# Layer norm's shift made on POOL, and work placed anew around the attention of a two-layer linear-attention and MLP kernel

## The chip, the cores and the metric

The kernel runs on one core of a Trainium2 chip. The core has a tensor engine (PE, with its weight loads PEld), a vector engine (DVE), a scalar engine (ACT), a general one (POOL) and a queue that issues most transfers (SP); each works through its own instructions in order, and they wait for each other by semaphores. The metric is the time of one execution in microseconds (us); of several runs, the median. Time before: 2634.08 us, median of 3 runs (2633.55 to 2637.23).

## The reference

Two layers, each an attention (A) and an MLP (B), both with a residual, with the same weights in both layers. S = 2048 rows, D = 576, H = 32 heads of Dh = 18, F = 4608, all in fp32.

```python
def _A_ref(x, wqkv, w_phi, wo):
    qkv = (x @ wqkv).reshape(B, S, 3, H, Dh).transpose(2, 0, 3, 1, 4)
    q, k, v = qkv[0], qkv[1], qkv[2]
    pq = jnp.einsum("bhsd,hdf->bhsf", q, w_phi)
    pk = jnp.einsum("bhsd,hdf->bhsf", k, w_phi)
    phi_q = concatenate([softmax(pq), softmax(-pq)])
    phi_k = concatenate([softmax(pk), softmax(-pk)])
    kv = jnp.einsum("bhsf,bhsd->bhfd", phi_k, v)
    z = jnp.einsum("bhsf->bhf", phi_k)
    num = jnp.einsum("bhqf,bhfd->bhqd", phi_q, kv)
    den = jnp.einsum("bhqf,bhf->bhq", phi_q, z)[..., None] + 1e-6
    return (num / den).transpose(0, 2, 1, 3).reshape(B, S, D) @ wo

def _B_ref(x, w1, b1, w2, b2):
    r = relu(x @ w1 + b1)
    return (r * r) @ w2 + b2

x = A_x
for layer in range(2):
    x = x + _A_ref(_layernorm(x), A_wqkv, A_w_phi, A_wo)
    x = x + _B_ref(_layernorm(x), B_w1, B_b1, B_w2, B_b2)
```

The attention isn't causal: the sums kv and z run over all 2048 rows, so no row's attention can be finished before the keys and values of every row are in.

## The kernel before

**Tiling.** The rows are cut into 4 blocks of 512, a block into 4 tiles of 128 rows (one row per partition). Products are made in three matmuls, of a high and a low piece of each fp32 operand (high by high, high by low, low by high); names end in h and l for them. PE writes into banks of its accumulators; ACT copies a result's high piece from there, and DVE subtracts it for the low one.

**Names.** A name's last number is left out in the profile. n_3m is the mean and variance of a tile of block 3 (blocks and tiles count from 0, over all blocks the tiles from 0 to 15), n_3d the inverse deviation, n_3b the shift (minus mean times inverse deviation), n_3n the normalised tile, n_3p its transpose in a bank, n_3h and n_3l the two pieces of the block's transposed rows. s0K9m is the peaks (largest and smallest per head) of the keys of tile 9, s0K9e the exponentials of both signs, s0K9r their sums. s010v is the values of tile 10, kvp the bank in which the sums over keys (kv) come together, zb the sums z spread over the partitions, t0q3Q0e to t0q3Q3e the query features of the last block's four tiles; t0ow0m and t0ow2m the products of these with zb for the first and second pair of tiles. Names with t1 or s1 are those of the second layer.

**A norm.** `Norm.stats` makes mean and variance on DVE (L353, L354) and the inverse deviation on POOL in two operations (L355, L356). `Norm.shift` makes the shift on DVE (L335). `scale_by_act` normalises on ACT (L344, L345) with shift and inverse deviation as its operands. `turn` transposes on PE (L380), ACT copies the high piece (L381), DVE makes the low one (L382); `rest` does the same for the last 64 columns of two tiles (L389 to L391).

**The stages**, with their places in the profile of before. *Fold* (0 to 44 us): the map w_phi is multiplied into the weights of queries and keys, while the four tiles of the first block are normalised. *Opening* (44 to about 240): for each of 16 tiles its keys (projection L421, copy L445, peaks L457 and L458, difference L471 with one half on DVE and one on POOL for the first twelve, exponentials L481 on ACT, sums L484, reciprocals L485, scaling L494), its values (L437; two columns of constants by memsets on POOL, L428 and L429), the sum of their product into kvp (L521), and the queries of the last block; beside them the norms of the remaining 12 tiles. *First barrier* (to about 308): the last keys, `key_totals` (z, L538 to L546), `key_blocks` (kv in block form, L557 to L571), the `Weights` of the first two tiles and of the other two (features times zb, L590; sums, L595; the denominator's reciprocal into the scaling, L600 to L603; scaling of the features, L494), the heads' products (L626 to L652), the projection with wo (L670, L673) and the norm ahead of the MLP. Then the MLPs of all four blocks, with the attention of the other blocks and the keys of the next layer woven in (to 1440). *Between* (1440 to 1521): the rest of the second layer's keys, values and queries, by `between()`. *Second barrier* (to 1593), and the MLPs of the second layer to the end.

**What sets the order.** In these stages the order of PE, ACT, DVE and POOL is that in which the code calls the operations. In the opening and in between, a table sets it: `plan.on(slot, depth, call, ...)` puts a call into a slot; the slots are run through in order, and within a slot the calls with greater depth come first. Two slots make one unit, a projection in two halves of 288 columns (so a unit is k, v, q or p of one tile). `unit[...]` is the first slot of each, in the order of `line`. The barriers are written out in code; there `halves[i]()` are halves of projections of the following block's queries that give PE something to do. Banks are taken in turn by `wtile`, from the rest of them and those named in `spare`.

## Time and profile before

| | us |
|---|---|
| median of 3 runs | 2634.08 (2633.55 to 2637.23) |
| the profiled execution's own time | 2635.62 |
| its span, first to last instruction | 2633.9 |
| PE busy | 2550.1 (97%) |
| DVE busy | 1179.7 (45%) |
| ACT busy | 745.4 (28%) |
| POOL busy | 87.4 (3%) |
| mean granted clock of PE | 0.989 |

The profile is of one execution. The span leaves out 1.72 us ahead of the first and behind the last instruction. "Busy" counts only instructions that compute, and matmuls are pipelined, so PE at 97% need not be PE at its peak; the granted clock is the share of full speed that PE was given. In rows of the timeline the columns are start, duration, engine, line, operation, output<-inputs with their shapes, count, and in brackets how long the engine had been idle and who released it. In rows of the waits they are engine and operation that waits, whom it waited for, us in total, times, and the longest.

### The profile page before, as it was taken

The numbers are of one execution on the slowest core, as the hardware profiler recorded it, in microseconds if no ns is written. First come the engines' busy times: TensorE is split into PE (matmuls) and PEld (weight loads), VectorE is DVE, ScalarE is ACT, GpSimd is POOL, SyncE is SP. The second block draws the span as 40 slices with busy tenths as digits, with TensorE's granted clock in tenths as the row PEclk, the third lists the DMA queues.
The fourth block names the chain that finished last, engine by engine and source line by source line (L and its number), as shares of the span: only waits on it lengthen the run. The fifth ranks groups of instructions, "written<-read, shape, count | busy, mean of one in ns | idle before, by whom it ended". The sixth has DMA issues, their size and how long they took to land.

```text
span 2633.9 us, 37310 instructions
## 1 busy us (share of the span) xinstructions
PE 2550.1 (97%) x15300; PEld 2241.3 (85%) x15300; DVE 1179.7 (45%) x2017; ACT 745.4 (28%) x1278; POOL 87.4 (3%) x229
## 2 busy tenths in 40 slices
PE   8788899999999999999999989999999999999999
PEld 7788788889888888888888888888888888888887
DVE  5677785543553445434412666431263325432111
ACT  4333444332221222212222333312222222312221
POOL 2110100000000000000000000000000000000000
PEclk9899999999999999999999999999999999999999
DMA  9412386886765766566556226556744574456665
GB/s 303 133 47 72 134 299 230 274 300 204 251 206 179 242 226 205 189 219 198 175 196 212 65 84 193 173 164 201 259 160 148 191 264 152 161 180 223 196 198 170
DMA packets 161143, 505.47 MB, mean 192 GB/s; under 512 B 21334, under 2 KB 49526, under 8 KB 160974
## 3 DMA queue, kind: packets, MB, share of 16 engines
q1 hardware_dynamic: 160974, 503.10, 57.4%
q8 instruction: 121, 1.98, 0.3%
q14 instruction: 48, 0.39, 0.0%
HBM read 418.39 MB, written 84.64 MB: 191 GB/s over the span
## 4 chain that ended last, share of the span: by engine, by line
PE 87%; DVE 5%; ACT 2%; DMA 2%; POOL 1%; issue 1%; SPq 0%; DVEq 0%; ACTq 0%; POOLq 0%
PE m_0ph L795 9%; PE m_1ph L795 9%; PE m_2ph L795 9%; PE m_3ph L795 8%; PE m_0acc L821 7%; PE m_1acc L821 7%; PE m_2acc L821 7%; PE m_3acc L821 6%; PE m_1acc L813 2%; PE m_0acc L813 2%; PE m_2acc L813 2%; PE m_3acc L813 2%; PE a_2po L670 1%; PE a_0po L670 1%; DMA m_3rr<-in_B_w 1%
## 5 line engine op out<-in xcount | busy, mean ns | idle before, releaser
L795 PE MATMUL m_0ph<-a_0nh,m_0h 128*128 128x512 f32 x720 | 226.4, 396 | 0.0
L795 PE MATMUL m_2ph<-a_2nh,m_2h 128*128 128x512 f32 x720 | 225.7, 395 | 0.6 <-DMA m_2h<-dw 0.6
L821 PE MATMUL m_0acc<-m_0s,m_0hb 128*128 128x448 f32 x864 | 189.9, 368 | 0.0
L821 PE MATMUL m_3acc<-m_3s,m_3hb 128*128 128x448 f32 x864 | 189.6, 368 | 0.3 <-DVE m_3hb L805 0.3
L821 PE MATMUL m_1acc<-m_1s,m_1hb 128*128 128x448 f32 x864 | 189.5, 367 | 0.3 <-DVE m_1hb L805 0.3
L821 PE MATMUL m_2acc<-m_2s,m_2hb 128*128 128x448 f32 x864 | 189.6, 368 | 0.0
L821 PEld LDWEIGHTS m_1acc<-m_1s,m_1hb 128*128 128x128 f32 x864 | 161.6, 188 | 18.1 <-DVE m_1hb L805 0.5
L821 PEld LDWEIGHTS m_3acc<-m_3s,m_3hb 128*128 128x128 f32 x864 | 161.4, 188 | 17.5 <-PE m_3ph L795 0.5
L821 PEld LDWEIGHTS m_2acc<-m_2s,m_2hb 128*128 128x128 f32 x864 | 160.7, 188 | 16.0
L821 PEld LDWEIGHTS m_0acc<-m_0s,m_0hb 128*128 128x128 f32 x864 | 160.4, 188 | 15.4
L805 DVE CAST m_2hb<-m_2hr 128x512 fp32r<-128x512 f32 x72 | 30.8, 427 | 316.3 <-ACT m_2hr L802 315.9
L795 PEld LDWEIGHTS m_2ph<-a_2nh,m_2h 128*128 128x128 f32 x720 | 135.5, 188 | 31.2 <-issue 1.0
L795 PEld LDWEIGHTS m_0ph<-a_0nh,m_0h 128*128 128x128 f32 x720 | 135.5, 188 | 29.8
L805 DVE CAST m_1hb<-m_1hr 128x512 fp32r<-128x512 f32 x72 | 30.7, 427 | 269.3 <-ACT m_1hr L802 269.3
L801 ACT ACTIVATE m_2hr<-m_2ph,b1t 128x512 f32<-128x512 f32 x72 | 49.5, 688 | 352.3 <-PE m_2ph L795 346.4
L805 DVE CAST m_0hb<-m_0hr 128x512 fp32r<-128x512 f32 x72 | 30.8, 427 | 260.8 <-ACT m_0hr L802 260.4
L801 ACT ACTIVATE m_0hr<-m_0ph,b1t 128x512 f32<-128x512 f32 x72 | 49.6, 688 | 333.5 <-PE m_0ph L795 333.5
L801 ACT ACTIVATE m_1hr<-m_1ph,b1t 128x512 f32<-128x512 f32 x72 | 49.6, 688 | 322.8 <-PE m_1ph L795 322.8
L795 PE MATMUL m_3ph<-t0onh,m_3h 128*128 128x512 f32 (+1 forms) x380 | 116.7, 391 | 6.3 <-ACT m_3hr L801 3.5
L795 PE MATMUL m_1ph<-t1onh,m_1h 128*128 128x512 f32 (+1 forms) x380 | 115.7, 389 | 0.5 <-ACT t1onh L381 0.5
L795 PE MATMUL m_3ph<-a_3nh,m_3h 128*128 128x512 f32 x360 | 113.3, 396 | 0.4 <-DMA m_3h<-dw 0.4
L795 PE MATMUL m_0ph<-a_0nl,m_0h 128*128 128x512 f32 x288 | 113.1, 393 | 0.0
(1928 smaller groups left out, 5535.1 us busy)
## 6 DMA issues: line engine op xcount, KB each, us to landing
m_2h<-dw SPq DMA_DIRECT2D x72, 640.0 KB
m_0h<-dw SPq DMA_DIRECT2D x72, 640.0 KB
m_1h<-dw SPq DMA_DIRECT2D x72, 640.0 KB
m_2s<-dw SPq DMA_DIRECT2D x72, 576.0 KB
m_0s<-dw SPq DMA_DIRECT2D x72, 576.0 KB
m_1s<-dw SPq DMA_DIRECT2D x72, 576.0 KB
dw<-m_3h SPq DMA_DIRECT2D x36, 640.0 KB
m_3h<-dw SPq DMA_DIRECT2D x36, 640.0 KB
```

What stands on the lines that cost most here:

```text
L670: nc.tensor.matmul(pt[:, :HP], a, m[:w, g], start=(g == 0 and k == 0), stop=(g == NG - 1 and k == 2))
L795: nc.tensor.matmul(ph[:, cols], a, m, start=(k == 0), stop=(k == 3 * KC + 1))
L801: nc.scalar.activation(hr, ph, AF.Relu, bias=b1t[:, f : f + 1])
L805: nc.vector.tensor_copy(hh, hr)
L813: nc.tensor.matmul(acc[KC], a, m, start=(f == 0 and k == 0), stop=(f == NF - 1 and k == 2))
L821: nc.tensor.matmul(acc[t][:, :R], a[:, rows], m, start=(f == 0 and k == 0), stop=(f == NF - 1 and k == 2))
```

## The change

It has five parts.

1. `Norm.shift` runs on POOL instead of DVE. It is used in the fold and the opening (16 tiles), in both barriers (4 each) and in between (4).
2. In the opening, statistics of a tile come one slot later, its scaling one slot later and at a place behind other work of the slot, its transpose two slots later; the first four tiles likewise by less. The sum over keys of a tile comes one or two slots later.
3. In `key_blocks` the product for the last head of each quarter (kq) comes ahead of the two masked ones (ko).
4. In the barrier, the products of the second pair's features with zb are made on POOL, ahead of the first half's heads, the second of them into a spare buffer for exponents. Both sums then follow each other, and the projection of the second tile comes behind the weights.
5. In between, the banks are taken in another order; statistics and shifts are spread over slots 0 and 1 (before: all in 0), scaling stands in slots 2 and 4, transposes in slots 3 and 6, and the sums over keys come one slot later.

```diff
         def shift(self, t):
             mv, rstd = self.stat[t]
             nmr = sb.tile([P, 1], F32, tag="nmr", name=f"{self.name}b{t}")
-            nc.vector.tensor_scalar(nmr, mv[:, 0:1], rstd, -1.0, op0=ALU.mult, op1=ALU.mult)
+            nc.gpsimd.tensor_scalar(nmr, mv[:, 0:1], rstd, -1.0, op0=ALU.mult, op1=ALU.mult)
...
-        def product(self, i):
-            m = self.m[i] = sb.tile([P, 2, D], F32, tag="m", name=f"{self.name}m{i}", bufs=1)
-            nc.vector.tensor_mul(m, self.e[i], self.zb)
+        def product(self, i, engine=nc.vector, spare=False):
+            if spare:
+                m = new_e(f"{self.name}m{i}")
+            else:
+                m = sb.tile([P, 2, D], F32, tag="m", name=f"{self.name}m{i}", bufs=1)
+            self.m[i] = m
+            engine.tensor_mul(m, self.e[i], self.zb)
...
         for t in range(NT):
             out.load(t)
+        w = weights[1]
+        w.product(0, nc.gpsimd)
+        w.product(1, nc.gpsimd, True)
...
         heads(0, 2)
-        w = weights[1]
         norm = Norm(dst, f"{out.name}n")
         next(gen)
-        w.product(0)
         w.total(0)
-        x = out.project(0)
-        w.product(1)
         w.total(1)
-        out.project(1)
+        out.project(0)
         w.both()
         w.apply(0)
         w.apply(1)
+        out.project(1)
         heads(1, 2)
...
         for N in range(NT):
             plan.on(3 * N + 1, 2, stats, N)
-            plan.on(3 * N + 2, 3, scale, N)
-            plan.on(3 * N + 4, -1, turn, N)
+            plan.on(3 * N + 3, -1, scale, N)
+            plan.on(3 * N + 4, -2, turn, N)
...
-                plan.on(max(raw + 7, unit["v", T] + 2), 6, ks.add, T)
+                plan.on(max(raw + 7, unit["v", T] + (3 if T < 13 else 4)), 6, ks.add, T)
         for N in range(NT, NB * NT):
             at = unit["k", N - NT]
             plan.on(at - 4, 9, load_rows, N)
-            plan.on(at + 2, 0, stats, N)
-            plan.on(at + 3, 3, scale, N)
-            plan.on(at + 4, 7, turn, N)
+            plan.on(at + 3, 2.5, stats, N)
+            plan.on(at + 4, 3.5, scale, N)
+            plan.on(at + 6, -1, turn, N)
...
-        spare["tags"] = ["acc1", "acc2", "acc3", "acc4", "h"]
+        spare.update(tags=["h", "acc4", "acc1", "acc2", "acc3"], i=4)
...
-            plan.on(unit["p", t] + 2, 6, ks.add, ("p", t))
+            plan.on(unit["p", t] + 3, 6, ks.add, ("p", t))
...
-                plan.on(max(unit["k", t] + 8, unit["v", t] + 2), 6, ks.add, t)
+                plan.on(max(unit["k", t] + 8, unit["v", t] + 3), 6, ks.add, t)
         for t in range(NT):
-            plan.on(0, 8, norm.stats, t, rows[t])
-            plan.on(0, 8, norm.shift, t)
-            plan.on(0, 7, norm.scale_by_act, t) if t < 2 else plan.on(4, 7, norm.scale_by_act, t)
-            plan.on((3, 3, 5, 6)[t], -1, norm.turn, t)
+            plan.on(t // 2, 8, norm.stats, t, rows[t])
+            plan.on(t // 2, 8, norm.shift, t)
+            plan.on(2 + t // 2 * 2, -1, norm.scale_by_act, t)
+            plan.on(3 + t // 2 * 3, -1, norm.turn, t)
             if t % 2:
-                plan.on((3, 6)[t // 2], -2, norm.rest, t // 2)
+                plan.on(3 + t // 2 * 3, -2, norm.rest, t // 2)
```

What the table makes of it on DVE, in the turn of the keys of tile 9 in the opening. Before:

```order
L457 TENSOR_REDUCE s0K9m<-s0ks_1891 128x32
L458 TENSOR_REDUCE s0K9m<-s0ks_1891 128x32
L353 BN_STATS n_3s_1953<-x_13_1705 128x6 x2
L354 BN_AGGR n_3m_1954<-n_3s_1953 128x2
L335 TENSOR_SCALAR n_3b_1961<-n_3m_1954,n_3d_1955 128x1
L471 TENSOR_TENSOR s0K9e<-s0ks_1891,s0K9m 128x576
L382 TENSOR_TENSOR n_3l<-n_3p_1988,n_3h 128x4x128
L391 TENSOR_TENSOR n_3h<-n_3p_1995,n_3h 64x256
L484 TENSOR_REDUCE s0K9r<-s0K9e 128x64
```

And with the change:

```order
L457 TENSOR_REDUCE s0K9m<-s0ks_1882 128x32
L458 TENSOR_REDUCE s0K9m<-s0ks_1882 128x32
L382 TENSOR_TENSOR n_3l<-n_3p_1946,n_3h 128x4x128
L353 BN_STATS n_3s_1953<-x_13_1702 128x6 x2
L354 BN_AGGR n_3m_1954<-n_3s_1953 128x2
L471 TENSOR_TENSOR s0K9e<-s0ks_1882,s0K9m 128x576
L484 TENSOR_REDUCE s0K9r<-s0K9e 128x64
```

The shift has gone from the queue, and the low piece n_3l, which stood behind the statistics of tile 13 and was of the same tile, now stands ahead of them and is that of tile 12 (buffers of one name are told apart by the number behind it).

On DVE in the first barrier, from the last head of the first half to the weights of the second pair. Before:

```order
L652 TENSOR_TENSOR t0oolt<-t0opn_3220,t0ooh 72x256
L590 TENSOR_TENSOR t0ow2m_3255<-t0q3Q2e,zb_2961 128x1152
L595 TENSOR_REDUCE t0ow2u<-t0ow2m_3255 128x64
L673 TENSOR_TENSOR t0ox_3113<-t0opo_3259,t0ox_3113 128x288
L673 TENSOR_TENSOR t0ox_3113<-t0opo_3276,t0ox_3113 128x288
L590 TENSOR_TENSOR t0ow2m_3293<-t0q3Q3e,zb_2961 128x1152
L595 TENSOR_REDUCE t0ow2u<-t0ow2m_3293 128x64
L673 TENSOR_TENSOR t0ox_3115<-t0opo_3296,t0ox_3115 128x288
L673 TENSOR_TENSOR t0ox_3115<-t0opo_3313,t0ox_3115 128x288
L600 TENSOR_TENSOR t0ow2u<-t0ow2u,t0q3r 128x128
```

And with the change:

```order
L656 TENSOR_TENSOR t0oolt<-t0opn_3224,t0ooh 72x256
L599 TENSOR_REDUCE t0ow2u<-t0ow2m_3121 128x64
L599 TENSOR_REDUCE t0ow2u<-t0ow2m1e 128x64
L677 TENSOR_TENSOR t0ox_3113<-t0opo_3262,t0ox_3113 128x288
L677 TENSOR_TENSOR t0ox_3113<-t0opo_3279,t0ox_3113 128x288
L604 TENSOR_TENSOR t0ow2u<-t0ow2u,t0q3r 128x128
```

The two products with zb are no longer there (they stand in POOL's queue, ahead of the feed-forward's weight pieces), nor are the two additions of the second tile's projection, which stand behind the weights; the lines of the change are 4 higher from there on.

On POOL in between, from the norms of the last block to the values of the first tile. Before:

```order
L355 TENSOR_SCALAR n_lastd_12901<-n_lastm_12900 128x1
L356 TENSOR_TENSOR n_lastd_12901<-n_lastd_12901,mhalf 128x1
L355 TENSOR_SCALAR n_lastd_12911<-n_lastm_12910 128x1
L356 TENSOR_TENSOR n_lastd_12911<-n_lastd_12911,mhalf 128x1
L428 MEMSET s1('p', 0)v_12926 128x32
L429 MEMSET s1('p', 0)v_12926 128x13
```

And with the change:

```order
L335 TENSOR_SCALAR n_lastb_12887<-n_lastm_12880,n_lastd_12881 128x1
L355 TENSOR_SCALAR n_lastd_12891<-n_lastm_12890 128x1
L356 TENSOR_TENSOR n_lastd_12891<-n_lastd_12891,mhalf 128x1
L335 TENSOR_SCALAR n_lastb_12897<-n_lastm_12890,n_lastd_12891 128x1
L428 MEMSET s1('p', 0)v_12899 128x32
L429 MEMSET s1('p', 0)v_12899 128x13
L355 TENSOR_SCALAR n_lastd_12921<-n_lastm_12920 128x1
L356 TENSOR_TENSOR n_lastd_12921<-n_lastd_12921,mhalf 128x1
```

The memsets of the first values (s1('p', 0)v) stood behind the inverse deviations of all four tiles; now they stand behind those of two tiles and their shifts.

More of the change, by code (lines that the diff above doesn't have):

```diff
@@ L553, in key_blocks @@
         sums[layer]["kb"] = kbh, kbl
-        todo = []
+        own = sb.tile([P, KC * P], F32, tag="xn", name=f"kq{layer}")
+        own = own[:, : 2 * w].rearrange("p (s q f) -> p s q f", s=2, q=NQ)
+        nc.vector.tensor_mul(own, kv[:, :, HG].unsqueeze(2).to_broadcast([P, 2, NQ, DH]),
+                             quarter.unsqueeze(1).unsqueeze(3).to_broadcast([P, 2, NQ, DH]))
+        blocks, todo = own, []
         for s in range(2):
@@ L563, in key_blocks @@
             todo.append((own.rearrange("p q j d -> p (q j d)"), [k[:, s, : last * GW] for k in (kbh, kbl)]))
-        own = sb.tile([P, KC * P], F32, tag="xn", name=f"kq{layer}")
-        own = own[:, : 2 * w].rearrange("p (s q f) -> p s q f", s=2, q=NQ)
-        nc.vector.tensor_mul(own, kv[:, :, HG].unsqueeze(2).to_broadcast([P, 2, NQ, DH]),
-                             quarter.unsqueeze(1).unsqueeze(3).to_broadcast([P, 2, NQ, DH]))
         pt = wtile(f"kt{layer}2")
@@ L570, in key_blocks @@
         for s in range(2):
-            nc.tensor.matmul(p3[:, s], own[:, s].rearrange("p q f -> p (q f)"),
+            nc.tensor.matmul(p3[:, s], blocks[:, s].rearrange("p q f -> p (q f)"),
                              place.rearrange("p q d -> p (q d)"), start=True, stop=True)
```

## The prediction

> **What bounds the kernel now.** I read the page's busy shares first, then busy time stage by stage, then what the tensor engine waits for.
>
> ```profile
> span 2633.9 us, 37310 instructions
> PE 2550.1 (97%) x15300; PEld 2241.3 (85%) x15300; DVE 1179.7 (45%) x2017; ACT 745.4 (28%) x1278; POOL 87.4 (3%) x229
> ```
>
> PE is busy 97% of the span, so whatever is to be won is in the 83.8 us in which it idles and in stretches at a lower clock. The table by stage (columns: stretch, length, busy time of PE, of its weight loads, DVE, ACT, POOL, granted clock, DMA share, GB/s) shows where:
>
> ```profile
> 160.00:200.00 40.00, 35.13 (x494) 33.53 (x493) 29.16 (x44) 17.12 (x32) 6.00 (x21) 1.00 0.08 24
> 200.00:235.00 35.00, 30.76 (x388) 29.95 (x387) 30.59 (x39) 10.63 (x19) 0.00 (x0) 0.92 0.01 1
> 575.00:1440.00 865.00, 863.12 (x4897) 754.28 (x4896) 356.49 (x611) 217.37 (x356) 16.89 (x56) 1.00 0.62 209
> ...
> 99.00:107.00 8.00, 5.99 (x85) 5.58 (x86) 5.12 (x7) 3.57 (x7) 0.73 (x2) 0.57 0.36 87
> 276.50:284.50 8.00, 5.90 (x27) 5.42 (x28) 5.28 (x9) 2.80 (x8) 0.00 (x0) 0.57 0.71 210
> 1450.50:1458.50 8.00, 6.07 (x85) 6.00 (x86) 0.92 (x4) 0.41 (x1) 1.39 (x12) 0.57 0.13 48
> ```
>
> The long middle of a layer is PE alone (863.12 of 865 us at full clock): nothing the change does there can matter. The opening, the two barriers and the stretch between the layers are where PE waits, and three of those places also show the clock at 0.57. What PE waits for there:
>
> ```profile
> PE n_2p L380 <- ACT n_2n L344: 13.7, 4, 5.2
> PE n_1p L380 <- ACT n_1n L344: 7.2, 4, 2.4
> PE n_3p L380 <- ACT n_3n L344: 6.5, 4, 1.6
> PE fo L228 <- ACT ft L220: 5.0, 6, 1.7
> PE kvp L521 <- POOL s1('p', 0)v L429: 4.4, 1, 4.4
> PE t0opt L626 <- DVE t0q3Q2e L494: 3.8, 1, 3.8
> PE kvp L521 <- ACT s014v L437: 3.8, 1, 3.8
> PE t1opt L626 <- DVE t1qQ2e L494: 3.3, 1, 3.3
> PE kt L571 <- DVE kq L566: 3.1, 2, 1.6
> PE m_3ph L795 <- DVE t0onl L382: 3.0, 2, 2.5
> ```
>
> Each of these is touched by the change. The first three, 27.4 us, are the transposes of normalised tiles in the opening. One turn there (the keys of one tile, K9, with the norm of a tile further on), and the first and thirteenth turns' starts:
>
> ```profile
> 48.10 0.75 DVE L457 TENSOR_REDUCE s0K0m<-s0ks 128x32 f32<-128x576 f32 x1 [2.22 <-ACT s0ks L445]
> ...
> 157.90 0.75 DVE L457 TENSOR_REDUCE s0K9m<-s0ks 128x32 f32<-128x576 f32 x1
> ...
> 159.23 0.81 DVE L353 BATCH_NORM_STATS2 n_3s<-x 128x6 f32<-128x288 f32 x2
> 160.07 0.21 DVE L354 BATCH_NORM_AGGREGATE n_3m<-n_3s 128x2 f32<-128x12 f32 x1
> 161.60 0.21 DVE L335 TENSOR_SCALAR n_3b<-n_3m,n_3d 128x1 f32<-128x1 f32 x1 [1.32 <-POOL n_3d L356]
> ...
> 164.04 0.69 DVE L382 TENSOR_TENSOR n_3l<-n_3p,n_3h 128x512 fp32r<-128x512 f32 x1 [1.56 <-ACT n_3h L381]
> 164.76 0.42 DVE L391 TENSOR_TENSOR n_3h<-n_3p,n_3h 64x256 fp32r<-64x256 f32 x1
> 165.36 1.35 DVE L484 TENSOR_REDUCE s0K9r<-s0K9e 128x64 f32<-128x1152 f32 x1 [0.17 <-ACT s0K9e L481]
> 168.68 0.75 DVE L457 TENSOR_REDUCE s0K10m<-s0ks 128x32 f32<-128x576 f32 x1
> 190.11 0.75 DVE L457 TENSOR_REDUCE s0K12m<-s0ks 128x32 f32<-128x576 f32 x1
> ```
>
> DVE's queue is in order, and it stands still twice in the turn: 1.32 us at the shift, for POOL's inverse deviation, and 1.56 us at the low piece L382, for a chain that starts with that shift and goes over ACT's scaling, PE's transpose and ACT's copy. PE stands in the same chain: its transpose waits for ACT's scaling. So the turn is a loop over four engines, not the work of one. It took 10.78 us here; twelve turns took 190.11 - 48.10 = 142.0, that is 11.83 each, and the first nine 12.2.
>
> **The change, part by part, with its cost.** *Opening.* The shift leaves DVE, and the scaling and transposes stand some slots later, so the low piece is that of a tile scaled in the turn before and needs no wait. DVE's turn is then a chain within one turn. The steps I price it from, ACT's and POOL's, and one that shows POOL delayed by DVE elsewhere:
>
> ```profile
> 161.85 0.81 ACT L344 ACTIVATE n_3n<-x,n_3b,n_3d 128x512 f32<-128x512 f32 x1 [2.13 <-DVE n_3b L335]
> ...
> 162.90 0.39 ACT L437 ACTIVATE s010v<-s010pv 128x288 f32<-128x288 f32 x1
> ...
> 164.16 1.16 ACT L481 ACTIVATE s0K9e<-s0K9e 128x1152 f32<-128x1152 f32 x1
> ```
>
> ```profile
> 160.70 0.22 POOL L355 TENSOR_SCALAR n_3d<-n_3m 128x1 f32<-128x1 f32 x1
> 161.00 0.57 POOL L356 TENSOR_TENSOR n_3d<-n_3d,mhalf 128x1 f32<-128x1 f32 x1
> ...
> 452.51 0.71 POOL L355 TENSOR_SCALAR a_2nd<-a_2nm 128x1 f32<-128x1 f32 x1 [153.86 <-DVE a_2nm L354]
> ```
>
> The same POOL operation takes 0.22 in the one row and 0.71 in the other, where a DVE product of two SBUF operands was running, and POOL's ended only with that. In the new order the instruction behind the aggregate on DVE is a key difference, also of two SBUF operands (about 0.75), so I hold POOL's first step for it. The new turn: peaks 1.33 (157.90 to 159.23); low pieces 0.69 and, in every second turn, 0.42: 0.90; statistics 0.84; from the aggregate to the scaling 2.0 (0.21, then 0.71 held, 0.57, a shift priced at 0.22 as the nearest one-column scalar operation, and the gaps between engines; bound 0.57 if it costs what the power does); ACT's scaling 1.05 (161.85 to 162.90), which now stands ahead of the exponential; exponential to sum 1.20; sum to the next peaks 3.32 (165.36 to 168.68). Together 10.64. Twelve turns are 127.7, less 0.9 (the first has no low piece), plus 2.6 for two pieces of the output weights that stay in DVE's queue (estimate): 129.4. The gain is **12.6**. Below, it is bounded by nothing (the loop keeps its pace, since K9's own turn, 10.78, is hardly longer than 10.64); above, by the 27.4 us of waits and what the clock lost behind them.
>
> PE's work in a turn is 35.13/40 of 10.74 (the mean of the last three), 9.4 us at full clock, so PE waits on DVE 1.2 us in each new turn, at the sum over keys, behind DVE's scaled exponentials. Behind the 1.6 us waits of n_3 the clock stayed at 1.00 (160 to 200); behind the 5.2 it was 0.57 (99 to 107). I take it to stay full.
>
> From K12 on the queries' units share DVE: it idles 4.4 of 35 us at 200 to 235. I take half, 2.3, since the low piece of the last tile now falls into K12's turn. The tail holds PE's wait of 3.8 for the last values and a clock of 0.92; with the two last value units ahead of that sum, I take 4 (bounds 0 and 3.8 + 0.08 x 35 = 6.6). Opening: 12.6 + 2.3 + 4 = **19**.
>
> By the Trainium skill ("SBUF — State Buffer", section "Who interferes with whom") a DVE instruction with two SBUF inputs and a POOL instruction that reads SBUF exclude each other for the whole instruction, and whoever starts first has the port. It speaks against putting more onto POOL; the trace agrees, 0.71 against 0.22 above and 1.79 against 1.35 below. Without it the result would be that of the second rival.
>
> *Folding, ahead of the opening.* The same shift, four tiles:
>
> ```profile
> 15.98 0.21 DVE L335 TENSOR_SCALAR n_0b<-n_0m,n_0d 128x1 f32<-128x1 f32 x1 [1.00 <-POOL n_0d L356]
> ```
>
> DVE gives back 1.00 + 0.21 in each, 4 x 1.21 = **4.8**; the stages behind it are short of DVE in every tile (bounds: 0 if ACT or the first loads hide it, 5.0 by the waits for ft).
>
> *First barrier.* The second half's two products go to POOL, ahead of the first half's heads; the key difference product kq goes ahead of the two masked ones; the two additions of one projection go behind the weights.
>
> ```profile
> 244.75 0.29 ACT L546 ACTIVATE zb<-z 128x144 f32<-128x144 f32 x1 [0.23 <-PE z L544]
> ...
> 248.20 1.35 DVE L590 TENSOR_TENSOR t0ow0m<-t0q3Q0e,zb 128x1152 f32<-128x1152 f32 x1
> ...
> 269.60 1.43 POOL L774 TENSOR_TENSOR m_3s<-m_3rr,m_3s 128x576 fp32r<-128x576 f32 x1
> ...
> 270.46 1.79 DVE L590 TENSOR_TENSOR t0ow2m<-t0q3Q3e,zb 128x1152 f32<-128x1152 f32 x1
> 273.55 0.95 DVE L673 TENSOR_TENSOR t0ox<-t0opo,t0ox 128x288 f32<-128x288 f32 x2
> ```
>
> POOL needs 1.43 for 576 elements with two operands, so some 2.65 for 1152 (estimate; 2.86 by doubling). Two of them from zb's end at 245.04 last to about 250.4. They hold DVE's own first product from 248.20 to 250.4: a **loss of 2.2** (bounds: 0 if DVE gets in between, 2.7 if both products are longer). In DVE's queue ahead of the second half's weights go 1.35 + 1.79 of products and 0.95 of additions. The heads of the second half start 4.1 - 2.2 = 1.9 earlier; PE's wait of 3.8 falls to 1.9, and with it the low clock of 276.5 to 284.5: PE's 5.90 busy us at 0.57 would be 3.4 at full clock, of which I take 2.0, DVE and ACT being in step there. Then the four norms behind: four shifts off DVE's queue shorten the wait for t0onl (3.0) by about 1.5, and its low clock by 0.6. Together **6** (3 to 9). kq ahead saves PE its wait of 1.6, but what PE does then early waits for the held product: nothing (bound 1.6).
>
> *Between the layers.* PE's sum over the first keys waits 4.4 us for two memsets that stand in POOL's queue behind four tiles' inverse deviations. In the new order they stand behind two, and the sum itself is one unit later; I take the wait whole. Its clock goes with it: 6.07 busy us at 0.57 in 1450.5 to 1458.5 are 3.4 at full, 2.6 saved. The banks' new order and the later sums save about 3 more (estimate: 0.9 at the first value unit and two waits of about 1 at the other sums): **10** (5 to 12).
>
> *Second barrier.* As the first, with a wait of 3.3 instead of 3.8: **5.5** (3 to 8). Its memsets and weight pieces on POOL are fewer, so I scale it by the wait.
>
> *Costs elsewhere.* POOL gains 28 shifts and four products, 28 x 0.22 + 4 x 2.65 = 17 us on 87.4 busy: covered by an idle engine. The second product needs a spare exponent buffer, which the sum over the last keys frees, and zb is worked out from that sum: no new wait. Behind the products in POOL's queue stand weight pieces of the feed-forward (269.60 is one), and POOL is through by 250.4: nothing. DVE's instructions in the long middle don't change.
>
> Sum: 4.8 + 19 + 6 + 10 + 5.5 = **45.3**. The profiled execution took 2635.62 (span 2633.9 and 1.72 around it), so 2590.3; the median of the runs shown is 1.54 lower, so **2589**.
>
> **Rivals.** *POOL is not held.* If POOL's step passes beside DVE's, 0.6 per turn (12 times: 7.2) and the barriers' 2.2 (twice: 4.4) come on top: 45.3 + 11.6 = 56.9, **2577**. For it: at 160.70 the same step took 0.22. Against: 452.51 and 270.46.
>
> *The opening keeps its pace.* The loop over DVE, POOL, ACT and back was 10.78 in K9's turn, and the new one is as long with the shift on POOL between the two. Then the 12.6 fall away: 32.7, **2601**. For it: that turn. Against: the earlier turns are 1.4 longer, and their PE waits were for n_1n and n_2n.
>
> *It does nothing where it counts.* Folding is bound by the first loads, the barriers by PE and ACT, and the waits only change name: within 5 us, **2632**. Against: four separate places would have to fail.
>
> *Slower: the clock falls in the opening.* Now PE has one stall per turn at the sum over keys. Should stalls of that kind (1.2, up to 2.6 with POOL held) bring the clock to 0.5, PE's 9.4 us per turn become 18.8, 8.2 above DVE's 10.64. Six such turns cost 49 and eat the whole gain; that is the point from which it decides. Eight, the likelier number since the last ones had full clock: 8 x 8.2 = 66, less 45, +20, **2654**; all twelve +53, 2687. For it: 0.57 behind the waits of 5.2 and 3.8. Against: clock 1.00 with waits of 1.6 each turn.
>
> The Trainium skill ("TensorE: Matmul & The Clock Gate", Part 1) has the clock drop after an idle window of about 3.4 us; by it a stall of 1.2 us brings nothing down, and the rows above agree.
>
> **How the numbers follow.** The forecast has 0.62 (its own range 2574 to 2604: the sum of the bounds, weighed), POOL not held 0.15, the opening's pace 0.15, nothing 0.03, slower 0.05. Range 2573 to 2612, which takes in the first three with some room above for terms sized too high. A measurement of this kernel can't tell 0.2%, 5.3 us, from no change: faster 0.62 + 0.15 + 0.15 = 0.92, same 0.03, slower 0.05.
>
> **What would show it.** Opening: L335 on POOL, no wait of PE for n_1n, n_2n, n_3n above 1 us, K0's to K12's peaks 129 us apart, clock 1.00 from 60 to 200. L355 at 0.7 there says that POOL is held; 0.22, that it isn't. First barrier: two POOL products of about 2.65, DVE's first product ending near 251.7 less the opening's gain, the wait for t0q3Q2e about 1.9. Between: no wait for memsets. Wrong: turns of 11.8 still, or a clock of 0.5 to 0.6 in them.

## The result and the profile after

| | before | after |
|---|---|---|
| median | 2633.82 us (4 runs, 2631.66 to 2637.23) | 2594.62 us (4 runs, 2592.06 to 2598.42) |
| the profiled execution | 2635.62 | 2592.06 |
| its span | 2633.9 | 2590.1 |

The ratio is 0.9851, with a 95% interval of 0.9834 to 0.9868: 39 us faster, where 45 were forecast (2589, range 2573 to 2612). The two profiled executions differ by 43.8 us in span, since that of the changed kernel was the fastest of its four and that of before was 1.8 us above its median. The stages below are from these two.

The page of the changed kernel, first its busy times:

```profile
span 2590.1 us, 37314 instructions
PE 2529.3 (98%) x15300; PEld 2222.6 (86%) x15300; DVE 1175.1 (45%) x1985; ACT 741.8 (29%) x1278; POOL 108.9 (4%) x261
```

POOL has its 32 operations more and DVE 32 fewer (28 shifts and four products); PE has as many matmuls as before, and is busy 20.8 us less, at a mean granted clock of 0.996 instead of 0.989. By stretches (columns as before: stretch, length, busy PE, weight loads, DVE, ACT, POOL, clock, DMA share, GB/s):

```profile
25.00:34.00 9.00, 7.25 (x59) 7.02 (x60) 4.97 (x11) 6.78 (x18) 3.17 (x8) 1.00 0.79 257
100.00:157.00 57.00, 49.14 (x661) 47.66 (x659) 38.48 (x57) 24.58 (x51) 13.73 (x30) 1.00 0.28 95
...
233.00:240.00 7.00, 5.79 (x30) 5.34 (x31) 4.49 (x9) 3.07 (x9) 0.00 (x0) 0.58 0.31 121
1507.00:1514.00 7.00, 5.91 (x34) 5.46 (x34) 4.78 (x11) 3.37 (x10) 0.00 (x0) 0.64 0.12 51
1450.00:1490.00 40.00, 40.00 (x537) 39.15 (x536) 27.82 (x37) 15.10 (x27) 0.00 (x0) 1.00 0.39 142
...
44.00:110.00 66.00, 58.67 (x778) 57.04 (x777) 44.95 (x67) 28.00 (x56) 16.77 (x37) 0.97 0.67 237
```

The opening runs at full clock now from 100 to 157 (and at 0.97 from 44 to 110, the last row), but PE is still idle in it for 7.9 of 57 us. In between the layers, PE is not idle at all from 1450 to 1490. Two stretches are at a low clock, and they are the starts of the two barriers' first heads, where there was none before. What PE waits for in the changed kernel:

```profile
PE t0opt L630 <- DVE t0q3Q0e L494: 5.4, 1, 5.4
PE t1opt L630 <- DVE t1qQ0e L494: 5.4, 1, 5.4
...
PE n_0p L380 <- ACT n_0n L344: 3.8, 4, 1.3
PE kvp L521 <- DVE s0K3e L494: 2.3, 1, 2.3
...
PE t0opt L630 <- DVE t0q3Q2e L494: 1.6, 1, 1.6
PE fo L228 <- ACT ft L220: 1.6, 4, 0.5
```

The 27.4 us for n_1n, n_2n and n_3n are gone. In their place stand 1.2 to 2.3 us per turn at the sum over keys (the row for s0K3e is the longest of ten), and two waits of 5.4 for the first pair's scaled features, which did not exist before.

One turn of the opening, of the same keys as before, with the starts of the first and thirteenth (the whole timeline, in order of time):

```profile
40.40 0.75 DVE L457 TENSOR_REDUCE s0K0m<-s0ks 128x32 f32<-128x576 f32 x1 [2.22 <-ACT s0ks L445]
...
137.32 0.75 DVE L457 TENSOR_REDUCE s0K9m<-s0ks 128x32 f32<-128x576 f32 x1
...
140.09 0.21 DVE L354 BATCH_NORM_AGGREGATE n_3m<-n_3s 128x2 f32<-128x12 f32 x1
140.21 0.70 DVE L471 TENSOR_TENSOR s0K9e<-s0ks,s0K9m 128x576 f32<-128x576 f32 x1
140.39 0.61 POOL L355 TENSOR_SCALAR n_3d<-n_3m 128x1 f32<-128x1 f32 x1 [0.22 <-DVE n_3m L354]
141.08 0.57 POOL L356 TENSOR_TENSOR n_3d<-n_3d,mhalf 128x1 f32<-128x1 f32 x1
141.76 0.27 POOL L335 TENSOR_SCALAR n_3b<-n_3m,n_3d 128x1 f32<-128x1 f32 x1
142.06 0.81 ACT L344 ACTIVATE n_3n<-x,n_3b,n_3d 128x512 f32<-128x512 f32 x1 [6.11 <-POOL n_3b L335]
...
143.11 1.15 ACT L481 ACTIVATE s0K9e<-s0K9e 128x1152 f32<-128x1152 f32 x1
...
144.36 1.35 DVE L484 TENSOR_REDUCE s0K9r<-s0K9e 128x64 f32<-128x1152 f32 x1 [3.44 <-ACT s0K9e L481]
...
168.77 0.74 DVE L457 TENSOR_REDUCE s0K12m<-s0ks 128x32 f32<-128x576 f32 x1
```

POOL's first step ends with DVE's difference (0.61 instead of 0.22), as the forecast had it, and DVE then stands idle for 3.44 us: for ACT's exponential, which had been possible since about 141 but stood in ACT's queue behind the scaling, and this waited for POOL. Twelve turns take 168.77 - 40.40 = 128.4 us (forecast 129.4).

Stage by stage, from the same landmarks in both traces (the opening is split at the peaks of K12; "zb" is the start of its last copy; "MLP" is the first matmul on the last block's normalised rows):

| stretch | before | after | gain | forecast |
|---|---|---|---|---|
| start to K0's peaks (folding) | 48.1 | 40.4 | 7.7 | 4.8 |
| K0's to K12's peaks | 142.0 | 128.4 | 13.6 | 12.6 |
| K12's peaks to zb | 54.6 | 47.6 | 7.0 | 6.3 |
| zb to MLP (first barrier) | 52.5 | 53.8 | -1.3 | 6 |
| MLP to the second layer's first values | 1146.5 | 1143.8 | 2.7 | 0 |
| from there to its zb (in between) | 86.2 | 76.3 | 9.9 | 10 |
| zb to MLP (second barrier) | 52.7 | 51.3 | 1.4 | 5.5 |
| to the end | 1051.3 | 1048.6 | 2.7 | 0 |

So both barriers came in below the forecast, together by some 11 us by these landmarks. Of the first one's 6, though, 2.1 were for the norms behind it, and these mostly fall behind the landmark MLP, into the next row. The first barrier's own rows, from the timeline of all engines:

```profile
226.55 2.68 POOL L594 TENSOR_TENSOR t0ow2m<-t0q3Q2e,zb 128x1152 f32<-128x1152 f32 x1 [56.56 <-DVE t0ow0u L599]
226.76 2.55 DVE L605 SCALAR_TENSOR_TENSOR t0ow0u<-t0ow0u 128x64 f32<-128x64 f32 x1
229.19 2.61 POOL L594 TENSOR_TENSOR t0ow2m1e<-t0q3Q3e,zb 128x1152 f32<-128x1152 f32 x1
229.34 0.55 DVE L606 RECIPROCAL t0ow0u<-t0ow0u 128x64 f32<-128x64 f32 x1
229.93 2.01 DVE L607 TENSOR_TENSOR t0q3r<-t0q3r,t0ow0u 128x128 f32<-128x128 f32 x1
...
233.48 0.45 PE L630 MATMUL t0opt<-ident,t0q3Q0e 128*126 128x128 f32 x1 [5.44 <-DVE t0q3Q0e L494]
```

POOL's first product does not start with zb (216.4) but ten microseconds later, released by DVE's sum of the first pair's second product (L599): both pairs' products share one buffer, which is free only then. It lands beside DVE's two smallest operations of the denominator, which take two operands from SBUF: 0.23 became 2.55 and 0.29 became 2.01 (the short ones are of the experiment "The products later", below), each ending with POOL's product. The reciprocal between them, with one operand, took its usual 0.55. By the Trainium skill ("SBUF — State Buffer", section "Who interferes with whom") a DVE instruction with two SBUF inputs and a POOL instruction that reads SBUF block each other, each for its whole length; the trace agrees, here with POOL ahead and DVE blocked.

In between, the memsets are done before PE asks for them, and the wait of 4.4 is gone (timeline of the changed kernel):

```profile
1418.53 0.16 POOL L428 MEMSET s1('p', 0)v<- 128x32 f32 x1
...
1419.92 0.77 PE L521 MATMUL kvp<-k_0K0e,s1('p', 0)v 128*32 128x36 f32 x64
```

### The profile page after: what moved, and what is told of

Its sections match the earlier page's. It is cut to its first block, busy times and chain, and to the rows that moved or that the text cites. A ratio compares the mean times of both kernels' runs of the same rounds, so it can differ in the third digit from the quotient of the medians.

```text
span 2590.1 us, 37314 instructions
## 1 busy us (share of the span) xinstructions
PE 2529.3 (98%) x15300; PEld 2222.6 (86%) x15300; DVE 1175.1 (45%) x1985; ACT 741.8 (29%) x1278; POOL 108.9 (4%) x261
## 4 chain that ended last, share of the span: by engine, by line
PE 85%; DVE 6%; ACT 2%; DMA 2%; issue 1%; POOL 1%; SPq 0%; DVEq 0%; ACTq 0%
PE m_1ph L799 9%; PE m_0ph L799 9%; PE m_2ph L799 9%; PE m_3ph L799 7%; PE m_1acc L825 7%; PE m_0acc L825 7%; PE m_2acc L825 7%; PE m_3acc L825 6%; PE m_1acc L817 2%; PE m_0acc L817 2%; PE m_2acc L817 2%; PE m_3acc L817 2%; DMA m_3rr<-in_B_w 2%; PE a_2po L674 1%; PE a_0po L674 1%
```

## The experiments

The theory after the result (A): in the opening the gain is that of the table, and the shift's place on POOL costs there; in the barriers POOL's products hold DVE. The rival (B): the gain is the time that the shift, and the products, no longer take on DVE. Stage times in the text are from the same landmarks as above.

### The shift back on DVE

```diff
-            nc.gpsimd.tensor_scalar(nmr, mv[:, 0:1], rstd, -1.0, op0=ALU.mult, op1=ALU.mult)
+            nc.vector.tensor_scalar(nmr, mv[:, 0:1], rstd, -1.0, op0=ALU.mult, op1=ALU.mult)
```

> The changed kernel with only the shift back on DVE (the new table, barriers and in-between kept). Theory A (the gain of the opening is that of the table, which took the low piece out of the loop over four engines): in K9's turn of the changed kernel the scaling starts 1.97 us behind the aggregate's start (140.09 to 142.06), since POOL's first step is held to 0.61 by DVE's difference. With the shift on DVE right behind the aggregate nothing runs beside POOL, so 0.22 + 0.57 + 0.21 and the gaps, about 1.4: each turn about 0.5 shorter, 12 turns -6; folding +4.8 (up to 8), the barriers +1.5 each, in between +0.5. Together 0 to +5: 2594 to 2600, K0 to K12 122 to 129 us. Theory B (the gain is that of the shift having left DVE): 28 shifts, each 1.2 us of DVE's time, come back: 20 to 30 us slower, 2615 to 2625, K0 to K12 143.

Measured: 2601.67 us (2599.79 to 2604.36), 7 slower than the changed kernel, just above theory A's range and far from theory B's. The two halves of it go opposite ways. K0 to K12 takes 121.9 us, 6.5 less than with the shift on POOL (expected: 6), but folding takes 47.7 instead of 40.4, 7.3 more, the upper end of what was expected for it. The timeline of the turn of K9:

```profile
142.60 0.22 POOL L355 TENSOR_SCALAR n_3d<-n_3m 128x1 f32<-128x1 f32 x1 [0.23 <-DVE n_3m L354]
...
143.51 0.21 DVE L335 TENSOR_SCALAR n_3b<-n_3m,n_3d 128x1 f32<-128x1 f32 x1 [1.00 <-POOL n_3d L356]
143.64 0.75 DVE L471 TENSOR_TENSOR s0K9e<-s0ks,s0K9m 128x576 f32<-128x576 f32 x1
143.75 0.82 ACT L344 ACTIVATE n_3n<-x,n_3b,n_3d 128x512 f32<-128x512 f32 x1 [5.07 <-DVE n_3b L335]
...
145.99 1.35 DVE L484 TENSOR_REDUCE s0K9r<-s0K9e 128x64 f32<-128x1152 f32 x1 [1.60 <-ACT s0K9e L481]
```

DVE waits 1.00 for the shift and 1.60 for the exponential, together less than the 3.44 of the changed kernel: while it stands at the shift it holds nothing, and POOL's step is 0.22. So the opening's gain isn't that of the shift having left DVE. In folding the shift's move is worth 7.3 with this table (4.0 in the old one, as the third experiment shows). In between the layers, the stage takes 77.0 with the shift back on DVE (76.3 in the changed kernel, 86.2 before), so the table gains nearly all of the 9.9 there without the shift's move.

### The opening's old table, the shift on POOL

```diff
-            plan.on(3 * N + 3, -1, scale, N)
-            plan.on(3 * N + 4, -2, turn, N)
+            plan.on(3 * N + 2, 3, scale, N)
+            plan.on(3 * N + 4, -1, turn, N)
...
-                plan.on(max(raw + 7, unit["v", T] + (3 if T < 13 else 4)), 6, ks.add, T)
+                plan.on(max(raw + 7, unit["v", T] + 2), 6, ks.add, T)
...
-            plan.on(at + 3, 2.5, stats, N)
-            plan.on(at + 4, 3.5, scale, N)
-            plan.on(at + 6, -1, turn, N)
+            plan.on(at + 2, 0, stats, N)
+            plan.on(at + 3, 3, scale, N)
+            plan.on(at + 4, 7, turn, N)
```

> The changed kernel with the opening's table of before (statistics, scaling, transposes, sums over keys), the shift still on POOL. Theory A (the loop): DVE's low piece waits again for a chain that starts in the same turn, now over POOL's shift too: K0 to K12 140 to 146 us instead of 128.4, low clock again; 2606 to 2615. Theory B (the shift's engine alone gains there): K0 to K12 128 to 132, 2594 to 2599.

Measured: 2628.68 us (2625.03 to 2630.29), 34 slower than the changed kernel, worse than theory A had it. K0 to K12 takes 151.8 us: not only the 13.6 come back, 9.8 more are lost against the kernel before. The timeline of the turn of K9:

```profile
162.60 0.21 DVE L354 BATCH_NORM_AGGREGATE n_3m<-n_3s 128x2 f32<-128x12 f32 x1
162.73 1.04 DVE L471 TENSOR_TENSOR s0K9e<-s0ks,s0K9m 128x576 f32<-128x576 f32 x1
163.35 0.49 POOL L355 TENSOR_SCALAR n_3d<-n_3m 128x1 f32<-128x1 f32 x1
...
164.60 0.27 POOL L335 TENSOR_SCALAR n_3b<-n_3m,n_3d 128x1 f32<-128x1 f32 x1
164.90 0.81 ACT L344 ACTIVATE n_3n<-x,n_3b,n_3d 128x512 f32<-128x512 f32 x1 [2.65 <-POOL n_3b L335]
...
167.09 0.69 DVE L382 TENSOR_TENSOR n_3l<-n_3p,n_3h 128x512 fp32r<-128x512 f32 x1 [3.33 <-ACT n_3h L381]
```

DVE no longer waits at the shift, but it waits 3.33 for the low piece (1.56 before), which is more than the 1.32 at the shift that it saved: the loop is as it was, and longer. From the aggregate to ACT's scaling it takes 2.30 here (162.60 to 164.90) and took 1.78 before (160.07 to 161.85); 0.27 of this 0.5 is POOL's held step. The mean turn is 0.8 longer than before; where the other 0.3 comes from is open. I had expected it to be at its old length. Against the changed kernel these turns lose 23.4 us. Of the rest, 3.4 are in folding, whose first tiles have their old table too, and 4.2 in the tail: K15's peaks to zb take 17.7 instead of 13.5, with the wait of 3.8 for the last values in it again.

### The shift on POOL alone, in the kernel before

The first edit's opposite, and nothing else of the change.

> The kernel before with nothing but the shift moved to POOL. Theory A (in the old table the shift is a link of the loop, and on POOL it stands behind operations that DVE's difference holds): folding 4 us faster, K0 to K12 about 152 us instead of 142.0 (as with the old table in the changed kernel, 151.8), the barriers 1.5 faster each, in between 1.4 slower: together +0 to +6, 2634 to 2640. Theory B (DVE's 1.2 us per shift are the gain): 28 times 1.2, 2600.

Measured: 2632.58 us (11 runs, 2631.33 to 2634.56), ratio 0.9991 (0.9982 to 1.0000): not to be told from no change, and just below theory A's range. Folding is 4.0 faster, K0 to K12 takes 153.7, 11.7 more than before, both as expected. The barriers, expected 1.5 faster each, take 52.4 and 53.4 (52.5 and 52.7 before), and the two long stretches are 2.8 and 2.7 shorter. In between was expected 1.4 slower and is 3.3 faster (from the first value unit to the last sum over keys; 2.3 of it shows in this row of PE's waits):

```profile
PE kvp L521 <- POOL s1('p', 0)v L429: 2.1, 1, 2.1
```

It was 4.4 before. DVE no longer stops at each shift, so the four statistics come to POOL sooner; that this is the whole reason was not tested.

### The table of in between as before

The last part of the diff undone, the shift on POOL.

> The changed kernel with the table of in between as it was before (banks, statistics, scaling, transposes, sums), the shift on POOL. Theory A (the gain there, 9.9 us from the second layer's first value unit to the last sum over keys, is the table's, through the memsets and the sums): all of it lost, and the memsets stand behind four shifts more, 4 x 0.35: 9 to 13 slower, 2603 to 2608. Theory B (the shift off DVE gains there): 2594 to 2598.

Measured: 2603.47 us (2601.16 to 2605.80), 9 slower, at the lower end of theory A. From the first value unit to zb it takes 82.8 us instead of 76.3: on top of the shift, the table is worth 6.5 of the 9.9, and the shift alone had brought 3.3. The other way round, the table alone brings 9.2 (77.0 with the shift back on DVE) and the shift 0.7 on top of it. Both take time off the same wait for the memsets (4.4 before, 2.1 with the shift alone, gone with the table), so their shares do not add up, and theory B's part exists only where the table is missing. Elsewhere, 2.0 and 1.5 more are lost at the two barriers, and 1.9 at folding, where nothing was edited (K0's peaks come at 40.3 to 42.3 in the traces with the changed kernel's folding).

### The second pair's products on DVE again

The barrier's order of before, the shift still on POOL and kq still ahead.

> The changed kernel with the barrier of before (products of the second pair on DVE, projections where they were), kq's earlier place and everything else kept. Theory A (on POOL the products start late, behind the buffer that the first pair's total frees, and hold two small DVE operations to 2.55 and 2.01 us, which costs what they save): no clear difference, 2590 to 2598; from zb to the norm's statistics 43 to 46 us (45.0 in the changed kernel). Theory B (the move gained the 5.5 to 6 us per barrier that the prediction gave it, and something else lost it): 11 slower, 2606.

Measured: 2593.25 us (2591.93 to 2594.20), no difference that could be told; from zb to the norm's statistics 45.0 in both, in the first barrier (43.4 against 42.5 in the second). On balance the four products on POOL won nothing. But two things cancel: with the products on DVE the first heads start 13.1 behind zb instead of 17.1, and from there to the MLP it takes 40.7 instead of 36.7. So the move did gain some 4 us behind the first heads, and the hold ahead of them cost as much.

### The products later

```diff
         w = weights[1]
+        gate = sb.tile([P, 1], F32, tag="nmr", name=f"{out.name}g")
+        nc.gpsimd.tensor_scalar(gate, queries.e[1][:, 1, D - 1 :], 0.0, None, op0=ALU.add)
         w.product(0, nc.gpsimd)
         w.product(1, nc.gpsimd, True)
```

> The changed kernel with one POOL operation on one column put ahead of the two products; it reads the last scaled feature of the first pair, so the products begin only when DVE has scaled it, beside heads whose DVE operations read one operand from a bank. Theory A (the hold is the loss): DVE's two small operations are 0.23 and 0.29 again, the first heads start 4 us earlier, PE's wait of 5.4 for them falls to 1.4 and the clock behind it stays up: 4 to 6 us in each barrier, 2583 to 2587. Theory B (PE or ACT sets the pace behind, the wait only moves): within 2.5 us of the changed kernel. If the products were then too late for their sums, the second heads would start later than 62 us behind the first product's start and it would be slower.

Measured: 2584.62 us (2583.54 to 2585.44), 10.0 faster than the changed kernel, as theory A had it. From its timeline, the first barrier:

```profile
226.54 0.23 DVE L605 SCALAR_TENSOR_TENSOR t0ow0u<-t0ow0u 128x64 f32<-128x64 f32 x1
...
227.39 0.29 DVE L607 TENSOR_TENSOR t0q3r<-t0q3r,t0ow0u 128x128 f32<-128x128 f32 x1
...
230.68 2.63 POOL L594 TENSOR_TENSOR t0ow2m<-t0q3Q2e,zb 128x1152 f32<-128x1152 f32 x1
```

The products are as long, 2.63, and hold nothing: beside them run the heads, whose operations on DVE read one operand from a bank. The first heads start 4.0 us earlier behind zb, PE's wait for them falls from 5.4 to 1.3, the first barrier takes 4.3 us less (zb to MLP) and the second 5.1. The clock behind the first heads was 0.86 from 228 to 240 in the first barrier and 1.00 from 1499 to 1511 in the second. A product on POOL costs what it runs beside.

### The products at zb

```diff
-        w.product(0, nc.gpsimd)
+        w.product(0, nc.gpsimd, True)
         w.product(1, nc.gpsimd, True)
```

> The changed kernel with both POOL products in spare exponent buffers, so that the first no longer waits for the first pair's total and both start at zb, as the prediction had it. Theory A (the hold falls on whichever DVE operation of two operands runs beside them): POOL from zb's end for 5.3 us, DVE's first product about 2.5 us late instead of 4.0 us at the two small operations: the first heads 1.5 us earlier than in the changed kernel, 1.5 to 3 us per barrier, 2588 to 2592, and slower than with the products behind the scaling (2584.6). Theory B (DVE gets in between, no hold): as fast as that, 2585.

Measured: 2592.16 us (2591.13 to 2592.56): 2.5 faster than the changed kernel by the medians, with ranges that overlap, and 7.5 slower than with the products later: the upper end of what theory A had. This is the arrangement that the prediction had in mind, and the length of its hold was nearly right, by its timeline:

```profile
216.59 2.65 POOL L594 TENSOR_TENSOR t0ow2m0e<-t0q3Q2e,zb 128x1152 f32<-128x1152 f32 x1 [46.71 <-ACT zb L546]
...
219.44 3.66 DVE L594 TENSOR_TENSOR t0ow0m<-t0q3Q0e,zb 128x1152 f32<-128x1152 f32 x1
...
231.58 0.30 PE L630 MATMUL t0opt<-ident,t0q3Q0e 128*126 128x128 f32 x1 [3.70 <-DVE t0q3Q0e L494]
```

DVE's first product took 3.66 instead of 1.35: 2.3 us of hold (forecast 2.2). But PE stands still for 3.70 at the first heads because of it, with a clock of 0.58 from 232 to 240, and the first barrier takes 53.7 (zb to MLP), as long as in the changed kernel; the second takes 49.5, 1.8 less.

### DVE's difference ahead of the statistics

```diff
-            plan.on(at + 3, 2.5, stats, N)
+            plan.on(at + 3, 1.5, stats, N)
```

> The changed kernel with DVE's key difference ahead of the statistics in the opening (before: behind the aggregate), the shift on POOL and the exponential where the change has it. Theory A (POOL's first step is held by that difference, and the scaling and the exponential wait for it): L355 at 0.22 instead of 0.61, from the aggregate to the scaling 1.5 instead of 1.97, K0 to K12 122 to 125 instead of 128.4, 4 to 6 us faster, 2588 to 2591. Theory B (the 0.61 comes from POOL's own start): L355 stays at 0.5 to 0.6 and the time within 2 us.

Measured: 2603.58 us (2601.92 to 2605.11), 9 slower where 4 to 6 faster were expected. The timeline of the turn of K9:

```profile
144.63 1.42 DVE L471 TENSOR_TENSOR s0K9e<-s0ks,s0K9m 128x576 f32<-128x576 f32 x1
...
147.12 0.22 POOL L355 TENSOR_SCALAR n_3d<-n_3m 128x1 f32<-128x1 f32 x1 [1.56 <-DVE n_3m L354]
...
150.70 1.35 DVE L484 TENSOR_REDUCE s0K9r<-s0K9e 128x64 f32<-128x1152 f32 x1 [3.68 <-ACT s0K9e L481]
```

The cause was right: with the difference out of the way POOL's step is 0.22. The sum was wrong: the difference now stands ahead of the aggregate, and there it is itself held, by POOL's own half of the difference (1.42 instead of 0.70). The aggregate starts 4.1 us behind the peaks (142.71) instead of 2.8, and K0 to K12 takes 136.1.

### The exponential ahead of the scaling

```diff
-            plan.on(at + 4, 3.5, scale, N)
+            plan.on(at + 4, 2.5, scale, N)
```

> The changed kernel with one number of the opening's table changed: ACT's exponential of the turn's keys ahead of the scaling of the next tile (before: behind it). Theory A (DVE's 3.44 us of idle time per turn, and PE's 1.3 to 2.3 behind it, come from the exponential standing behind a scaling that waits for POOL's held shift): DVE's wait falls to about 1.2, PE's 17 us of waits at the sums over keys go, and PE's own work, 8.6 to 9.4 us, becomes the turn: K0 to K12 110 to 117 us instead of 128.4, 12 to 17 faster, 2578 to 2583. Theory B (the scaling is then late for its transpose, or ACT's order holds the next keys): K0 to K12 over 124, within 4 us of 2594.6.

Measured: 2575.07 us (2571.66 to 2576.48), 19.6 faster than the changed kernel, more than theory A's 12 to 17. K0 to K12 takes 107.2 us, below what was expected. DVE's wait in the turn of K9, 3.44 in the changed kernel, is 1.30 in this timeline:

```profile
128.13 1.17 ACT L481 ACTIVATE s0K9e<-s0K9e 128x1152 f32<-128x1152 f32 x1 [2.04 <-POOL n_3d L355]
...
128.87 0.27 POOL L335 TENSOR_SCALAR n_3b<-n_3m,n_3d 128x1 f32<-128x1 f32 x1
129.20 0.80 ACT L344 ACTIVATE n_3n<-x,n_3b,n_3d 128x512 f32<-128x512 f32 x1
129.33 1.35 DVE L484 TENSOR_REDUCE s0K9r<-s0K9e 128x64 f32<-128x1152 f32 x1 [1.30 <-ACT s0K9e L481]
```

The exponential starts as soon as DVE's difference is there (the row names POOL's first step, which the difference holds and which ends with it), ahead of POOL's shift at 128.87 instead of behind it. The scaling is not late for that: it starts at 129.20, just behind the shift. Only one wait at a sum over keys is left above 1 us.

### Both together

The exponential first, and the products behind the first pair's scaling.

> The exponential first in the opening, and the products behind the first pair's scaling, both in the changed kernel. The two act in different stages, so theory A has their gains add: 10.0 from the products (measured: 2584.62 against 2594.62) and 12 to 17: 2568 to 2573. Theory B of the run before: 2581 to 2585.

Measured: 2564.66 us (2564.22 to 2564.93), ratio to before 0.9737 (0.9723 to 0.9752): 68 us faster than before in the same series, 30 faster than the change, and faster than the 2568 to 2573 expected. The two add: 10.0 + 19.6 = 29.6. The same stretch of the opening as in the changed kernel, in the same columns:

```profile
100.00:157.00 57.00, 57.00 (x781) 55.75 (x780) 48.69 (x72) 28.90 (x55) 15.55 (x39) 1.00 0.21 67
```

PE is busy throughout, 8.93 us for a turn; what any of the other engines does in these turns no longer shows in the time.

## Why the prediction was right, and where it wasn't

**The whole.** 45.3 us were forecast, against the profiled execution; the profiled ones differ by 43.8, the medians by 39. That the sum came so near was in part luck: by the table, folding, the opening and the long stretches came out 10 higher than forecast, and both barriers 11 lower.

**Opening, right.** The turn came out at 10.70 us (forecast 10.64), with POOL's step held (0.61, forecast 0.71) and PE waiting at the sum over keys as foreseen, at 1.2 to 2.3 instead of 1.2. The sentence "the loop keeps its pace" as a lower bound was the old table's property: with it and the shift on POOL, the loop was slower still, 151.8. What the prediction did not say is that the shift's move works against the table here: with the shift on DVE the same table gives 121.9. Which of the table's moves counts most was not separated. PE's work in a turn was taken from a stretch that also holds the first queries, 9.4; it is at most 8.93. From K12 to zb 7.0 were gained (forecast 6.3, where half of 4.4 was entered as 2.3 instead of 2.2); PE's wait for the last values, 3.8 before, is 0.6 there.

**Folding, too small.** 7.7 instead of 4.8. The term "4 x 1.21" was near for what it priced: in the kernel before, the shift alone gives 4.0. The rest is the first four tiles' new places in the table, which the prediction put at nothing, and they pay only together with the shift's move: with the shift back on DVE they gave 0.4 (47.7 against 48.1). PE's wait in the fold for ACT's copies of the turned weights (fo for ft) shows the same: 5.0 before, 1.6 with the change, 6.9 with the shift back on DVE. Why the two need each other was not tested. PE was at half speed from 25 to 34 us before (columns as in the stretches above):

```profile
25.00:34.00 9.00, 8.14 (x35) 7.26 (x36) 4.68 (x13) 5.86 (x17) 3.88 (x6) 0.50 0.66 217
```

The same stretch ran at 1.00 after, but also with the shift back on DVE, where folding was nearly as long as before; so this clock alone does not explain the gain. Runs with the same folding differ by up to 2.

**First barrier, wrong.** The step that failed is "Two of them from zb's end at 245.04 last to about 250.4", and with it the "loss of 2.2". The first product waited for a buffer, not for zb alone, and the hold of 2.2 on one product became one of 4.0 on two small operations ahead of the first heads. There it opened a wait of PE of 5.4 us and a stretch at a clock of 0.58, which the sum had at nothing. The second half's heads, forecast "1.9 earlier", so came later: they start 36.1 behind zb instead of 33.1 (heads to heads 19.8 before, 19.0 after; the first heads 3.8 later). The buffer is only part of the error: with both products at zb, as that step has it, zb to MLP took 53.7 and 49.5, 1.2 more and 3.2 less than before, since PE's wait of 3.7 at the first heads and the low clock behind it remain.

With the products behind the scaling, and so without the hold, it takes 49.5 and 46.2, which is 3.0 and 6.5 less than before; in the first barrier the second heads are then 1.3 earlier, where the sum had 4.1 before it took off the hold. So the gain in DVE's queue was put too high there as well. Of the claim that PE's wait for the second pair falls, the number was right: 1.6 (forecast 1.9), and the low clock behind it (0.57 before) is gone, with 1.00 from 248 to 264. The earlier place of kq was not tested by itself; with it and the products on DVE the first heads start 13.1 behind zb instead of 13.3, so it is worth next to nothing here, as forecast.

**Second barrier.** Scaled from the first, and wrong with it: 1.4 to the MLP instead of 5.5.

**In between, right.** 9.9 for 10; the wait for the memsets went whole. The prediction gave nearly all of it to the table, and the table alone, with the shift on DVE, does bring 9.2. The shift alone brings 3.3, of the same wait; only 0.7 of that is left beside the table.

**Long stretches, foreseen in part.** They gained 2.7 us each. 1.5 for a shorter wait for the last low pieces (t0onl), and 0.6 of clock behind it, were in the first barrier's sum, and the wait did fall, from 3.0 to 1.2. It is 1.2 with the shift alone too, and 2.9 with the shift back on DVE, so this is the shift's doing. The two traces with the shift on DVE are also the longest in both stretches: from the first MLP matmul to the second layer's first values 1146.5 and 1146.7, against 1141.9 to 1145.7 in the other ten; to the end 1051.3 and 1052.8, against 1048.4 to 1050.5. With a spread that wide among the ten, how much of the 2.7 is the shift's is not settled.

**Rivals.** "POOL is not held" falls: 0.61 in the opening, and DVE's 2.55 and 2.01 (its price of 0.6 per turn was high: 0.71 less 0.22 is 0.5). "The opening keeps its pace" falls with the table, and holds without it. "Slower: the clock falls in the opening" falls: ten waits of up to 2.3 us left the clock at 1.00 from 100 to 157, and at 0.97 from 44 to 110. "It does nothing where it counts" falls with the 39 us.

## What to carry to other kernels

Moving a small operation to an idle engine pays where the first engine stood still for it (folding) and costs where the other engine is held by the first one's instructions; the same edit gave 7.3 us in one stage and took 6.5 in the next. Two edits that shorten the same wait do not add up, and two that need each other are worth more together: undo each of them alone before you share out the gain. Before a product is put on POOL, look at what releases it, buffers included, and at which DVE instructions with two SBUF operands will run beside it: the same two products cost 4 us, 2.3 us or nothing, by their start alone. When a stage got faster, look for the engine that still stands idle in its turn and the instruction ahead of the one it waits for: one number in ACT's order was worth half of the whole change again.

## What the runs showed of the hardware

A small DVE instruction with two SBUF operands, 0.23 us by itself, took 2.55 when it started 0.2 us behind a POOL product, and one with a single operand in between was untouched (0.55). The hold goes both ways within one turn: POOL's 0.22 became 0.61 beside DVE's difference, and DVE's 0.70 became 1.42 beside POOL's. Ten idle gaps of PE of 1.2 to 2.3 us, one per turn of about 10.7, left the granted clock at or near full (1.00 from 100 to 157, 0.97 from 44 to 110). Gaps of 5.4 had 7 us at 0.58 and 0.64 behind them, one of 3.7 had 8 us at 0.58, and the one of 3.8 before had 8 us at 0.57. Short gaps are not always harmless: with the products later, two of 1.3 and 0.9 us within 2.6 us had a clock of 0.50 from 232 to 234 behind them.
